# One decode step of a gated attention and MLP block: the first load of wq as two transfers, of 16 and of 112 partitions

## The chip, the cores and the metric

The kernel runs on one core of a Trainium2 chip. The time of a run is in device microseconds, from launch to end on that core. Beside the times of plain runs there is one execution taken by the hardware profiler, with a trace of every instruction and of every data transfer.

## The reference

For two batch rows of one token each, the reference mixes an attention block over a long cache with a small MLP block by a gate:

```
x = A_x                                               # (2, 1, 1024)
g = sigmoid((x * gate_w).sum(-1, keepdims=True))
q = (x @ wq)                                          # wq (1024, 4096): 32 heads of 128
scores = q . k_cache * 128 ** -0.5                    # 4 kv heads, 32768 keys each, 8 q heads to a kv head
a = (softmax(scores) . v_cache) @ wo                  # wo (4096, 1024)
hs = spatial shift of gelu(layernorm(x) @ w1) @ w2    # one token: every shift moves it out, hs = 0
b = x1 + gelu(layernorm(x1) @ w3) @ w4, x1 = x + hs   # w3 (1024, 3584), w4 (3584, 1024)
out = g * a + (1 - g) * b
```

All numbers are 32-bit floats. The two caches are 134 MB each, wq and wo 16.8 MB each, w3 and w4 14.7 MB each. Each of these bytes is used once.

## The kernel before

The kernel is a stream of large loads into two buffers, `bufs[0]` and `bufs[1]` (line 86), each of 128 partitions by 16,384 floats, so 64 KiB (65,536 bytes) in each partition. One load fills one buffer, and loads alternate between the two. There are 40 of them: two each for wq, w3 and w4, then for each of the eight pairs of a kv head and a batch row two of keys (`kt`) and two of values (`vt`), and two of wo. A load of wq, kt, vt or wo is 128 rows of 65,536 bytes, 8.4 MB; one of w3 or w4 has rows of 57,344 bytes.

All these loads are issued by SyncE (SP). The helper `load(i, src, needs)` (lines 469 to 473) makes SP wait until TensorE (PE) has done the work `needs` on what lay in the buffer, and then issues one transfer, which raises the semaphore `landed[i % 2]` by 16 when all of it has landed. The loop of lines 475 to 490 calls it with i = 0, 1, 2 and so on. The loads 0 and 1 (both of wq) wait for nothing. Line 491 calls it once more for the first load of wo, with the literal 0 for i, since that load goes into `bufs[0]`. The second load of wo is written out in lines 492 to 498: five transfers of 8, 4, 2, 1 and 1 sixteenths of the columns, each with a semaphore of its own.

On PE, `take(sem, n)` (line 131) waits for a semaphore and counts it down again by n. `columns` (line 148) takes `landed` and then multiplies the buffer with x: one call for each load of wq and of w3. After the first has read the whole of `bufs[0]`, the event `load0` lets SP issue load 2. The loop over the eight pairs (line 213) takes `landed` before the scores and before the values of each half, lines 280 to 291 do so for wo. Ahead of the first `columns`, PE transposes x, sums for the gate and the layer norm, and puts x * (1 - g) into the accumulator `acc`, with `x16` loaded by a small transfer of 16 partitions from ScalarE's queue (line 140). VectorE (DVE) and ScalarE (ACT) do the softmax, the copies out of PSUM and the norm. At the end DVE copies `acc` (line 462) and SP stores it (line 500).

Of the kernel before, what the change touches and what calls it, by code (L numbers as in the profile page):

```python
# [57 lines left out]
def kernel(  # L58
# [11 lines left out]
    nc = tc.nc  # L70
    scale = DH ** -0.5

    def sbuf(name, cols, rows=P):
        return ctx.enter_context(nc.sbuf_tensor(name, [rows, cols], F32))[:, :]
# [4 lines left out]
    def at(t, offset, *dims, rows=(0, P)):  # L79
        width = t.ap[0][0]  # L80
        return bass.AP(t.tensor, t.offset + rows[0] * width + offset,
                       [[width, rows[1] - rows[0]], *[list(d) for d in dims]])
# [3 lines left out]
    bufs = [sbuf("buf0", RUN), sbuf("buf1", RUN)]  # L86
# [34 lines left out]
    with tc.tile_critical(no_gpsimd_drain=True):  # L121
        new = tc.alloc_semaphore
        landed = [new("landed0"), new("landed1")]
        pieces = [landed[1]] + [new(f"piece{i}") for i in range(1, len(PIECES))]
        edge, dvp, acp = new("edge"), new("dve_to_pe"), new("act_to_pe")
        dve, act = Line(nc.vector, new("dve")), Line(nc.scalar, new("act"))
        pool, sp = Line(nc.gpsimd, new("pool")), Line(nc.sync, None)
# [3 lines left out]
        def take(sem, n=1):  # L131
            t.wait_ge(sem, n).then_inc(sem, -n)  # L132

        def mm(o, lhsT, rhs, start, stop):
            return t.matmul(o, lhsT, rhs, start=start, stop=stop, skip_group_check=True)  # L135

        def quarter(t_, g):
            return t_[C * g:C * g + C]
# [6 lines left out]
        def mark(name, ins):  # L145
            events[name] = pe.did(ins)

        def columns(load, pad, n, banks):
            wide = n // G
            take(landed[load % 2], 16)  # L150
            for ek in range(E * E):
                for u, bank in enumerate(banks):
                    lo, hi = u * 512, min(u * 512 + 512, wide)
                    for g in range(G):
                        start = ek * n + g * wide
                        last = mm(quarter(bank, g)[:, :hi - lo], at(pad, ((load % 2) * 4 + ek) * C, (1, C)),
                                  bufs[load % 2][:, start + lo:start + hi],
                                  load % 2 == 0 and ek == 0, load % 2 == 1 and ek == 3)
            mark(f"load{load}", last)
# [19 lines left out]
        for e in range(E):  # L179
            for kk in range(E):  # L180
                for g in range(G):
                    lo, hi = halves[g % 2]
                    mm(quarter(acc, g), xr_pad[lo:hi, ((g // 2) * 4 + e * 2 + kk) * C:][:, :C],
                       place[lo:hi, P + 1 - P * kk - e:][:, :D // G], e == 0 and kk == 0, False)
        columns(0, x_pad, HQ * DH, sc[0:2])
        columns(1, x_pad, HQ * DH, sc[0:2])
        take(dvp)
# [214 lines left out]
        for half, (lo, hi) in enumerate(halves):  # L402
            for W in range(2):
                n = E * KT
# [64 lines left out]
        def load(i, src, needs):  # L469
            if needs:  # L470
                sp.wait(pe, needs)
            n = src.shape[1]
            nc.sync.dma_start(bufs[i % 2][:, :n], src).then_inc(landed[i % 2], 16)

        i = 0
        for src in (wq, w3, w4):
            for W in range(2):
                load(i, tiles(src, W), events[f"load{i - 2}"] if i > 1 else 0)
                i += 1
        for m in range(PAIRS):  # L480
            for kind, src in (("k", kt), ("v", vt)):
                for L in range(2):
                    if kind == "v":
                        needs = at_pair(m, f"scores{2 * L + 1}")
                    elif m:
                        needs = at_pair(m - 1, f"values{L}")
                    else:
                        needs = events[f"load{4 + L}"]
                    load(i, tiles(src[m], L), needs)
                    i += 1  # L490
# [42 lines left out]
```

## Time and profile before

| | |
|---|---|
| three plain runs, median (lowest to highest) | 777.53 us (777.21 to 777.81) |
| the profiled execution, its own time | 777.37 us |
| its span, first to last instruction | 775.6 us |
| read from HBM | 331.36 MB |
| busy: PE, DVE, ACT, POOL | 433.6, 71.5, 37.2, 4.1 us |
| mean granted TensorE clock | 0.75 |

The page counts the span in microseconds. Matmuls show under PE, the loads of their weights under PEld, and SPq and ACTq are the queues that issue transfers. In the windows, "DMA share" is the mean busy share of the 16 DMA engines and "GB/s" the bytes moved, both booked at the time at which a packet starts. So in windows shorter than a packet they show when packets start, not how fast they run. "x" and a number is a count. In the timeline, square brackets hold the idle time before a group and what ended it. In the order listings a row is an instruction with its shape, and "waits" names the semaphores that it waits for.

### The profile page before, as it was taken

The numbers are of one execution on the slowest core, as the hardware profiler recorded it, in microseconds if no ns is written. First come the engines' busy times: TensorE is split into PE (matmuls) and PEld (weight loads), VectorE is DVE, ScalarE is ACT, GpSimd is POOL, SyncE is SP. The second block draws the span as 40 slices with busy tenths as digits, with TensorE's granted clock in tenths as the row PEclk, the third lists the DMA queues.
The fourth block names the chain that finished last, engine by engine and source line by source line (L and its number), as shares of the span: only waits on it lengthen the run. The fifth ranks groups of instructions, "written<-read, shape, count | busy, mean of one in ns | idle before, by whom it ended". The sixth has DMA issues, their size and how long they took to land. (4 is left out here: it accounts for less than half of the span.)

```text
span 775.6 us, 8888 instructions
## 1 busy us (share of the span) xinstructions
PE 433.6 (56%) x4148; PEld 185.3 (24%) x4148; DVE 71.5 (9%) x203; ACT 37.2 (5%) x88; POOL 4.1 (1%) x14
## 2 busy tenths in 40 slices
PE   4454654483657364835484657464735484657365
PEld 3121231141213121412141213121312141214133
DVE  3000100020002000200020002000200020001000
ACT  1000100020002000200020002000200020002000
POOL 2000000000000000000000000000000000000000
PEclk9976676686679677867686679677967686679679
DMA  9999999999999999999999999999999999999996
GB/s 379 437 432 456 433 419 437 433 434 430 439 436 433 433 433 436 433 433 433 433 430 433 433 433 433 433 433 433 433 436 433 433 433 433 433 433 433 433 423 258
DMA packets 6397, 331.56 MB, mean 428 GB/s; under 512 B 728, under 2 KB 752, under 8 KB 1008
## 3 DMA queue, kind: packets, MB, share of 16 engines
q1 hardware_dynamic: 6352, 331.36, 98.9%
q8 instruction: 10, 0.16, 0.1%
q14 instruction: 3, 0.02, 0.0%
q10 hardware_dynamic: 32, 0.01, 0.0%
HBM read 331.36 MB, written 0.01 MB: 427 GB/s over the span
## 5 line engine op out<-in xcount | busy, mean ns | idle before, releaser
L135 PE MATMUL sc<-buf,q_cur 128*32 128x512 f32 x1024 | 150.7, 754 | 132.2 <-PEq L132 132.2
L135 PE MATMUL pv<-buf,pt 128*32 128x512 f32 x1024 | 133.9, 682 | 102.2 <-PEq L132 102.2
L135 PEld LDWEIGHTS sc<-buf,q_cur 128*32 128x32 f32 x1024 | 41.1, 135 | 235.7 <-issue 235.7
L135 PEld LDWEIGHTS pv<-buf,pt 128*32 128x32 f32 x1024 | 38.9, 123 | 184.2 <-issue 184.0
L417 DVE TENSOR_REDUCE mx<-sc 128x1 f32<-128x512 f32 x32 | 22.1, 691 | 292.8 <-PE sc L135 292.8
L430 ACT ACTIVATE p<-sc,bias 128x512 f32<-128x512 f32 x32 | 21.6, 685 | 563.6 <-DVE bias L427 563.6
L135 PE MATMUL tr<-ident,p 128*64 128x64 f32 x1024 | 43.0, 262 | 9.2 <-PEq L132 9.2
L135 PEld LDWEIGHTS tr<-ident,p 128*64 128x64 f32 x1024 | 42.1, 174 | 9.7 <-issue 9.7
L135 PE MATMUL tr<-sel,pv_sb 128*128 128x8 f32 x128 | 20.1, 294 | 12.0 <-PEq L132 12.0
L135 PE MATMUL sc<-buf,x_pad 128*32 128x512 f32 x128 | 17.5, 708 | 16.7 <-PEq L132 16.7
L450 DVE COPY pv_sb<-pv 128x512 f32<-128x512 f32 x16 | 10.3, 685 | 164.5 <-PE pv L135 164.5
L135 PE MATMUL acc<-buf,h_pad 128*32 128x256 f32 x224 | 16.1, 456 | 14.7 <-PEq L132 14.7
L135 PEld LDWEIGHTS tr<-sel,pv_sb 128*128 128x128 f32 x128 | 19.6, 241 | 19.0 <-issue 19.0
L135 PE MATMUL sc<-buf,xn_pad 128*32 128x384 f32 (+1 forms) x128 | 15.7, 654 | 14.3 <-PEq L132 14.3
L135 PE MATMUL acc<-buf,o_pad 128*32 128x256 f32 x256 | 16.7, 411 | 10.4 <-PEq L132 10.3
L135 PEld LDWEIGHTS acc<-buf,h_pad 128*32 128x32 f32 x224 | 8.9, 131 | 21.5 <-issue 18.6
L135 PEld LDWEIGHTS acc<-buf,o_pad 128*32 128x32 f32 x256 | 9.2, 118 | 17.5 <-issue 14.4
L135 PEld LDWEIGHTS sc<-buf,x_pad 128*32 128x32 f32 x128 | 4.9, 128 | 29.3 <-issue 29.3
L135 PEld LDWEIGHTS sc<-buf,xn_pad 128*32 128x32 f32 x128 | 5.0, 131 | 24.4 <-issue 24.4
L445 DVE RECIPROCAL norm<-tr 128x8 f32<-128x8 f32 x8 | 1.7, 207 | 66.9 <-PE tr L135 66.9
L433 DVE COPY pt<-tr 128x512 f32<-128x512 f32 x8 | 5.5, 691 | 20.6 <-PE tr L135 20.6
L227 PE MATMUL tr<-ident,m 128*1 128x128 f32 x8 | 2.2, 269 | 8.8 <-PEq L132 8.8
(78 smaller groups left out, 100.9 us busy)
## 6 DMA issues: line engine op xcount, KB each, us to landing
buf<-w SPq DMA_DIRECT2D x4, 7168.0 KB, 25.8
buf<-wo SPq DMA_DIRECT2D x1, 4096.0 KB, 20.4
buf<-wo SPq DMA_DIRECT2D x1, 2048.0 KB, 25.0
buf<-wo SPq DMA_DIRECT2D x1, 1024.0 KB, 27.0
buf<-wo SPq DMA_DIRECT2D x2, 512.0 KB, 28.1
buf<-kt SPq DMA_DIRECT2D x16, 29.8
buf<-vt SPq DMA_DIRECT2D x16, 29.1
buf<-wq SPq DMA_DIRECT2D x2, 32.2
```

Source lines behind the costliest of these rows:

```text
L135: return t.matmul(o, lhsT, rhs, start=start, stop=stop, skip_group_check=True)
L227: mark("mt", t.transpose(tr[0][:1, :P], m1[0], ident))
L417: dve.did(v.reduce_max(out=mx[i2][:, i:i + 1], in_=sc[i], axis=AX.X))
L430: act.did(s.activation(p_sb[i], sc[i], AF.Exp, bias=bias[i2], scale=scale, accum_out=l4[i2][:, i:i + 1]), acp)
L433: dve.did(v.tensor_copy(p_t[0], tr[0]), dvp)
L445: dve.did(v.reciprocal(norm, tr[0][:, :REP]))
L450: dve.did(v.tensor_copy(at(pv_sb, e * P, (E * P, G), (H, 2), (1, H)), at(pv, e, (P, G), (0, 2), (2, H))), dvp if e else None)
```

## The change

A new semaphore `first` is made. In `load`, the case i == 0 issues two transfers in place of one: partitions 0 to 15, which raises `first`, and partitions 16 to 127, which raises `landed[0]`. Ahead of the first `columns`, PE takes `first` as well. All other loads go as before.

```
+        first = new("first")
...
+        take(first, 16)
         columns(0, x_pad, HQ * DH, sc[0:2])
...
             n = src.shape[1]
+            if i == 0:
+                nc.sync.dma_start(bufs[0][:16, :n], src[:16]).then_inc(first, 16)
+                nc.sync.dma_start(bufs[0][16:, :n], src[16:]).then_inc(landed[0], 16)
+                return
             nc.sync.dma_start(bufs[i % 2][:, :n], src).then_inc(landed[i % 2], 16)
```

Line 491 of before also calls `load` with 0, so the condition holds there too.

SP's queue at the head of the program, before:

```order
L529 UNCONDITIONAL_BRANCH [waits SP_sequencer_49]
L473 DMA buf<-wq 128x16384 x2
L473 DMA buf<-w 128x14336 [waits pe] x4
L473 DMA buf<-kt 128x16384 [waits pe] x2
L473 DMA buf<-vt 128x16384 [waits pe] x2
```

The same place now (line numbers are those of the changed kernel):

```order
L535 UNCONDITIONAL_BRANCH [waits SP_sequencer_49]
L476 DMA buf<-wq 16x16384
L477 DMA buf<-wq 112x16384
L479 DMA buf<-wq 128x16384
L479 DMA buf<-w 128x14336 [waits pe] x4
```

The first of the two transfers of 128 partitions has become one of 16 and one of 112; the second stands behind them.

SP's queue at the end, where wo is loaded, before:

```order
L473 DMA buf<-wo 128x16384 [waits pe]
L496 DMA buf<-wo 128x8192 [waits pe]
L496 DMA buf<-wo 128x4096
L496 DMA buf<-wo 128x2048
L496 DMA buf<-wo 128x1024 x2
```

And now:

```order
L476 DMA buf<-wo 16x16384 [waits pe]
L477 DMA buf<-wo 112x16384
L502 DMA buf<-wo 128x8192 [waits pe]
L502 DMA buf<-wo 128x4096
L502 DMA buf<-wo 128x2048
```

The first load of wo is in two as well. Nothing takes `first` there.

## The prediction

> **What bounds the kernel now.** I read the page's head and its DMA rows first:
>
> ```profile
> span 775.6 us, 8888 instructions
> PE 433.6 (56%) x4148; PEld 185.3 (24%) x4148; DVE 71.5 (9%) x203; ACT 37.2 (5%) x88; POOL 4.1 (1%) x14
> DMA  9999999999999999999999999999999999999996
> q1 hardware_dynamic: 6352, 331.36, 98.9%
> ```
>
> No engine is near full. The 16 DMA engines are: SP's queue q1 keeps them busy for 98.9% of the span, and only the last of the 40 slices shows slack. The kernel is one stream of bytes, and what lengthens the stream lengthens the kernel. The chain of waits reaches back only over the last microsecond, so it says nothing here.
>
> Next, windows cut to a fraction of a microsecond at the start, and one long window of the middle (the last two columns are DMA share and GB/s):
>
> ```profile
> 1.90:2.90 1.00, 0.00 (x0) 0.00 (x0) 0.73 (x4) 0.73 (x1) 1.00 (x4) 1.00 3.16 1061
> 2.90:4.90 2.00, 0.00 (x0) 0.00 (x0) 2.00 (x4) 0.00 (x0) 2.00 (x5) 1.00 0.00 0
> 4.90:5.70 0.80, 0.34 (x2) 0.37 (x2) 0.54 (x5) 0.00 (x0) 0.18 (x1) 1.00 3.02 1311
> 5.70:7.30 1.60, 1.60 (x10) 1.60 (x9) 0.00 (x0) 0.00 (x0) 0.00 (x0) 1.00 0.00 0
> 7.30:8.10 0.80, 0.80 (x5) 0.80 (x6) 0.00 (x0) 0.00 (x0) 0.00 (x0) 1.00 3.02 1311
> ...
> 100.00:700.00 600.00, 338.92 (x3123) 139.37 (x3119) 55.71 (x150) 27.69 (x70) 0.00 (x0) 0.73 1.00 434
> ```
>
> Packets are booked where they start, and they start in waves. One wave is 0.80 us x 1311 GB/s = 1.05 MB, which is 16 rows of 65,536 bytes: one for each DMA engine. Between waves nothing starts. A row's pace comes from the wave's share: 3.02 x 0.80 us = 2.42 us that each engine spends on its row, and the next wave begins 2.4 us later. So there are 16 streams, each moving one row into one partition at a time, in 2.42 us. A load of 128 rows is eight waves, 8 x 2.42 = 19.4 us. In the long window the share is 1.00 at 434 GB/s, or 27.1 GB/s for each stream, and 65,536 bytes at that rate take 2.42 us again. The first wave begins at about 1.9 us, is 1.0 us wide, and its rows take longer (the second begins 3.0 us after it).
>
> Then the transfers from issue to landing; the first line is that of wq alone (least, median, most):
>
> ```profile
> DMA to landing us min/median/max: 21.9/32.2/42.4
> ...
> buf<-kt SPq DMA_DIRECT2D x16, 29.8
> buf<-vt SPq DMA_DIRECT2D x16, 29.1
> ...
> buf<-wo SPq DMA_DIRECT2D x1, 31.4
> ```
>
> A load in the middle lands 29 to 30 us after its issue, of which 19.4 us are its own rows. It stood about 10 us in the queue (12.0 us for the first of wo). The streams are always fed, with 10 us to spare.
>
> Last the two places that the change touches, in the timeline:
>
> ```profile
> 0.95 0.87 SPq L473 DMA_DIRECT2D buf<-wq  x2
> 23.01 8.85 PE L135 MATMUL sc<-buf,x_pad 128*32 128x512 f32 x64 [4.65 <-PEq L132]
> 31.93 0.33 SPq L473 DMA_DIRECT2D buf<-w  x1
> 43.92 1.94 PE L135 MATMUL sc<-buf,x_pad 128*32 128x512 f32 x8 [12.06 <-PEq L132]
> ...
> 718.75 0.33 SPq L473 DMA_DIRECT2D buf<-wo  x1
> 740.89 2.23 SPq L496 DMA_DIRECT2D buf<-wo  x5
> 750.33 8.75 PE L135 MATMUL acc<-buf,o_pad 128*32 128x256 f32 x128 [5.47 <-PEq L132]
> 768.85 1.86 PE L135 MATMUL acc<-buf,o_pad 128*32 128x256 f32 x24 [0.54 <-PEq L132]
> 771.32 0.64 PE L135 MATMUL acc<-buf,o_pad 128*32 128x256 f32 x8 [0.61 <-PEq L132]
> 772.02 0.42 DVE L462 COPY o_sb<-acc 128x256 f32<-128x256 f32 x1 [26.93 <-PE acc L135]
> ```
>
> PE waits for both loads of wq and for wo, down to the last piece, and what follows the last landing is 0.64 us of PE, 0.42 us of DVE and a store.
>
> **The change part by part.**
>
> *The cheap edits.* One more issue on SP costs about 0.43 us at the start (0.87 for two) and 0.33 us at wo. Behind it stand load 1 at the start, which has 19.4 us of rows ahead of it, and at wo the pieces of line 496, which wait for PE until 740.89 anyway. Without that cover an issue would cost its 0.3 to 0.4 us. The added take of `first` stands on PE where PE has already idled 4.65 us. Queued behind it are the 64 matmuls of load 0, then load 2's issue, which has 10 us to spare; a take with its wait costs at most 0.54 us (the smallest idle in the rows above), and nothing where the other transfer lands later. I count these at nothing.
>
> *The start.* Could 16 rows go off sooner than 128? The first wave is 1.0 us wide, and its rows take about 0.6 us more than 2.42. If every stream began at 1.90 and ran at full pace, the second wave's latest start, 5.70, would be 4.32: a gain of 1.4 us at the utmost. The waves keep their shape for the rest of the run, so this would arrive at the end in full. I take 0, since nothing in the rows ties the width of the first wave to the number of rows issued.
>
> *Where the rows go.* This decides. The bytes are the same, and 16 rows over 16 streams are one row each, 112 are seven each, in sum the eight of before. But in the wave of the first transfer all 16 streams write into 16 neighbouring partitions. No large transfer of before writes fewer than 128 partitions, so the trace can't say whether 2.42 us for a row is the pace of the stream that carries it or of the place into which it is written. Bounds for the transfer of 16: one row for each stream, 2.4 us, if the pace is the stream's own; 8 x 2.42 = 19.4 us, if the way in is divided evenly over the partitions (16 of 128 have two of sixteen shares, for sixteen rows). Between them lie four and eight shares, for 9.7 and 4.8 us. I take 9.7 us: four rows behind each other at each way in, near the middle of the doublings.
>
> [...]
>
> For the transfer of 112, bounds again: 7 x 2.42 = 16.9 us if no two streams ever meet at a way in, and twice that, 33.9 us, if each row shares it with another. Seven rows for a stream don't fall on the same borders as the eight of the full load, so I expect meetings, but not everywhere, and take the middle, 25.4 us.
>
> *The sum.* The first load: 9.7 + 25.4 = 35.1 us in place of 19.4, so 15.7 us more. Nothing hides it: the streams run at a share of 1.00 from then on, PE finishes load 0 later by as much, load 2 is issued later by as much, and the last stream never runs dry. Streams that came through sooner may run dry for a while, which costs nothing, since the latest stream sets the end. The first load of wo is split the same way, another 15.7 us, and the five pieces queue behind it. Both: 31.4 us. The profiled execution took 777.37 us around its span of 775.6; the median of the runs is 777.53, which I start from, as the two differ by 0.02%. 777.5 + 31.4 = 808.9, say **809 us**. By the lower bound of the second transfer a load costs 9.7 + 16.9 - 19.4 = 7.2 us, so 792 for both; by the upper 9.7 + 33.9 - 19.4 = 24.2 us, so 826.
>
> **The rivals.**
>
> *The pace is the stream's own (no change).* Then 2.4 + 16.9 = 19.4 us, as before, and 777.5 us is the time, give or take the 0.4 us of an issue. For it: the steady 27.1 GB/s of each stream, the same for rows of every load. Against: that is seen only where each load spreads over all partitions, where the two explanations look alike. It decides if the wave of 16 rows takes below about 3 us. Chance 0.21.
>
> *The start tightens (faster).* The pace is the stream's own, and besides, the streams start together because the first transfer has one row for each of them. Place: the first wave. Price: at most -1.4 us, so 776.1. This kernel's measurement can tell 0.2% from no change, which is 1.55 us; to be called faster the start would have to give more than the rows allow. It decides only if the first wave narrows from 1.0 us to almost nothing and its rows reach 2.42 us. Chance 0.04, for what I have not seen.
>
> *Neighbouring rows on neighbouring streams, all through.* If the transfer of 112 deals its rows out one at a time, then in each of its seven waves the 16 streams again write 16 neighbouring partitions: 7 x 9.7 = 67.9 us, 77.6 for the load, 58.2 more, and 116 for both: 894 us. For it: it is the simplest way to deal. Against: dealt so, the full loads of before would crowd the same way, and they run at 434 GB/s; only another dealing for 112 than for 128 would bring it. Chance 0.08.
>
> That the wo load stays whole is no rival: the order listing shows it as two.
>
> **How the numbers follow.** The forecast, a crowd at the way in at 7 to 24 us for each load, has a chance of 0.67, and its own range is 792 to 826. With the stream's own pace at 0.21, the range has to reach down to it: from 776.1 (the best start) to 826. Left out are the crowd all through (0.08) and the corner of a second transfer dearer than its upper bound. Faster: 0.04. Same: 0.21. Slower: 0.67 + 0.08 = 0.75.
>
> **What would show it.** In the profile after, the windows at the start: by the forecast, the second wave doesn't begin near 4.9 us but around 11 to 12, and the first matmul on wq near 39 us in place of 23.01. The transfer of 16 partitions would show some 10 us from start to landing. In the middle, 100 to 700 us, the share stays 1.00 or close and nothing else moves except by the delay. At the end the first matmuls on wo come another 10 to 25 us later against the last values. If the second wave begins near 4.9 us, the forecast is wrong at its root. If it begins at 11 us, but the first load lands by 31 us, then only the price of the 112 was too high. If the wo load lands without a delay of its own, the second term is wrong.

## The result and the profile after

| | before | after |
|---|---|---|
| median of plain runs (lowest to highest) | 777.38 us (777.10 to 777.81, 6 runs) | 825.68 us (824.15 to 826.56, 6 runs) |
| profiled execution: its time, its span | 777.37, 775.6 us | 824.88, 823.1 us |

The ratio is 1.0619, with a 95% interval of 1.0607 to 1.0630: 48.3 us slower. The forecast was 809, 31.4 us slower, in a range from 776 to 826. So the time lies inside the range, but 0.3 us from its end, and the slowest of the six runs lies beyond it.

The head of the page after, with the GB/s of the 40 slices (20.6 us each):

```profile
span 823.1 us, 8891 instructions
...
DMA  9999999999999999999999999999999999999995
GB/s 163 264 426 430 416 441 441 427 438 428 431 433 433 433 433 440 427 443 424 443 427 440 427 440 427 440 427 440 427 443 420 446 420 446 424 443 229 229 266 242
...
q1 hardware_dynamic: 6384, 331.36, 98.8%
```

The GB/s row of before, in slices of 19.4 us:

```profile
GB/s 379 437 432 456 433 419 437 433 434 430 439 436 433 433 433 436 433 433 433 433 430 433 433 433 433 433 433 433 433 436 433 433 433 433 433 433 433 433 423 258
```

The same 331.36 MB, a busy share of 98.8% where it was 98.9%, and yet 48 us more. The busy row hides the loss: a slow row counts as busy for as long as it takes (below, 8.5 us for a row of the first wave, where 2.42 us was the pace). The GB/s row shows it. After, the first two slices and the last four fall to between 163 and 266, and all between them run at some 430. Before, only the first and the last slice were low, at 379 and 258. Both loads that were split have their price, and nothing else has.

The windows at the start of after, cut to the waves (rows are booked where they start):

```profile
1.90:3.10 1.20, 0.00 (x0) 0.00 (x0) 0.93 (x4) 0.74 (x1) 1.20 (x5) 1.00 7.10 884
3.10:9.40 6.30, 3.57 (x16) 3.48 (x16) 2.69 (x7) 0.00 (x0) 1.98 (x4) 1.00 0.00 0
9.40:11.70 2.30, 0.58 (x3) 0.55 (x3) 1.18 (x8) 0.00 (x0) 0.00 (x0) 1.00 2.36 456
11.70:15.40 3.70, 1.21 (x10) 0.90 (x14) 0.86 (x5) 1.66 (x3) 0.00 (x0) 1.00 0.00 0
15.40:16.70 1.30, 1.30 (x16) 0.67 (x12) 0.00 (x0) 0.00 (x0) 0.00 (x0) 1.00 3.56 807
20.10:21.30 1.20, 0.00 (x0) 0.00 (x0) 0.00 (x0) 0.00 (x0) 0.00 (x0) 1.00 2.61 874
23.30:25.70 2.40, 0.00 (x0) 0.00 (x0) 0.00 (x0) 0.00 (x0) 0.00 (x0) 1.00 1.59 437
27.00:29.40 2.40, 0.00 (x0) 0.00 (x0) 0.00 (x0) 0.00 (x0) 0.00 (x0) 1.00 1.91 437
31.10:33.90 2.80, 0.00 (x0) 0.00 (x0) 0.00 (x0) 0.00 (x0) 0.00 (x0) 1.00 1.66 374
35.90:38.50 2.60, 0.00 (x0) 0.00 (x0) 0.00 (x0) 0.00 (x0) 0.00 (x0) 1.00 1.73 403
40.50:43.30 2.80, 0.00 (x0) 0.00 (x0) 0.00 (x0) 0.00 (x0) 0.00 (x0) 1.00 1.06 375
100.00:700.00 600.00, 330.83 (x3203) 139.61 (x3199) 57.02 (x162) 29.74 (x73) 0.00 (x0) 0.76 1.00 433
```

In each wave's window 16 rows start (GB/s x width is 1.05 MB), so share x width is the mean time of one row. The first wave, the 16 rows of the first transfer, starts within 1.2 us, and a row takes 7.10 x 1.20 = 8.5 us. The seven waves of the 112 take 5.4, 4.6, 3.1, 3.8, 4.6, 4.6 and 4.5 us, 30.7 us in sum. The last window is the first wave of load 1 at 3.0 us. Before, a row took 2.42 us (3.2 in the first wave). The middle is as before: a share of 1.00 at 433 GB/s.

Transfers from issue to landing (the first line is wq: the 16, the 112 and load 1), and the two places in the timeline:

```profile
DMA to landing us min/median/max: 12.1/42.9/61.8
...
buf<-kt SPq DMA_DIRECT2D x16, 30.1
buf<-vt SPq DMA_DIRECT2D x16, 29.5
```

```profile
1.41 0.42 SPq L477 DMA_DIRECT2D buf<-wq  x1
...
44.46 8.39 PE L136 MATMUL sc<-buf,x_pad 128*32 128x512 f32 x64 [26.09 <-PEq L133]
...
740.36 0.42 SPq L477 DMA_DIRECT2D buf<-wo  x1
...
799.60 13.17 PE L136 MATMUL acc<-buf,o_pad 128*32 128x256 f32 x192 [26.58 <-PEq L133]
820.00 0.70 SPq L506 DMA_DIRECT2D out<-o_sb  x1
```

The first matmul on wq starts at 44.46 in place of 23.01, 21.5 us later. The first on wo starts at 799.60 in place of 750.33, 49.3 us later. The 112 of wo took 59 us from issue to use, where the whole load took 31.6 us (718.75 to 750.33). Keys and values land in 30 us as before.

### The profile page after: what moved, and what is told of

Read it like the earlier page. It is cut to its first block, busy times and chain, and to the rows that moved or that the text cites. A ratio compares the mean times of both kernels' runs of the same rounds, so it can differ in the third digit from the quotient of the medians.

```text
span 823.1 us, 8891 instructions
## 1 busy us (share of the span) xinstructions
PE 422.5 (51%) x4148; PEld 181.3 (22%) x4148; DVE 71.5 (9%) x203; ACT 37.2 (5%) x88; POOL 4.1 (0%) x14
## 3 DMA queue, kind: packets, MB, share of 16 engines
q1 hardware_dynamic: 6384, 331.36, 98.8%
HBM read 331.36 MB, written 0.01 MB: 403 GB/s over the span
## 5 line engine op out<-in xcount | busy, mean ns | idle before, releaser
L136 PE MATMUL sc<-buf,q_cur 128*32 128x512 f32 x1024 | 144.6, 728 | 139.0 <-PEq L133 139.0
L136 PE MATMUL pv<-buf,pt 128*32 128x512 f32 x1024 | 129.7, 664 | 116.1 <-PEq L133 116.1
L432 ACT ACTIVATE p<-sc,bias 128x512 f32<-128x512 f32 x32 | 21.5, 685 | 564.0 <-DVE bias L429 564.0
L136 PE MATMUL tr<-sel,pv_sb 128*128 128x8 f32 x128 | 17.1, 269 | 12.0 <-PEq L133 12.0
L136 PEld LDWEIGHTS tr<-sel,pv_sb 128*128 128x128 f32 x128 | 16.6, 209 | 19.0 <-issue 19.0
L136 PEld LDWEIGHTS sc<-buf,xn_pad 128*32 128x32 f32 x128 | 5.1, 135 | 24.2 <-issue 24.2
L435 DVE COPY pt<-tr 128x512 f32<-128x512 f32 x8 | 5.5, 692 | 19.1 <-PE tr L136 19.1
L439 DVE COPY pt<-tr 128x512 f32<-128x512 f32 x8 | 5.5, 692 | 18.8 <-PE tr L136 18.8
```

What stands on the lines that cost most here:

```text
L432: act.did(s.activation(p_sb[i], sc[i], AF.Exp, bias=bias[i2], scale=scale, accum_out=l4[i2][:, i:i + 1]), acp)
L435: dve.did(v.tensor_copy(p_t[0], tr[0]), dvp)
L439: dve.did(v.tensor_copy(p_t[2], tr[0]), dvp)
```

## The experiments

Theory A is that of the prediction: rows of one wave crowd into too few ways in. Its rivals are B (only the tail hurts), C (more transfers cost time) and D (the side that is read is slow). All kernels start from the kernel before.

### One split at a time: wq_only and wo_only

```
 def load(i, src, needs, split=False): ...
+            if split:
+                nc.sync.dma_start(bufs[0][:16, :n], src[:16]).then_inc(first, 16)
+                nc.sync.dma_start(bufs[0][16:, :n], src[16:]).then_inc(landed[0], 16)
+                return
```

In wq_only, `split` is set for the first load of wq alone; in wo_only for the first load of wo alone, and PE takes `first` there.

> Only the first load of wq is split into 16 and 112 partitions; the first load of wo is one transfer, as before. Theory A (the rows of a wave crowd into too few partitions, and the streams stand behind each other where they write): the first load lands some 21 us later than the 22.9 us of before, as it does in the changed kernel, and the delay reaches the end whole: 777.4 + 21 = 798 us. Rival B (only the tail is hurt, since a delay at the start is caught up by the queue's 10 us of spare time): under 785 us. Rival C (the price is that of more transfers in the queue, not of partitions): the same 21 us, so this run doesn't tell A from C.

> Only the first load of wo is split into 16 and 112 partitions, and TensorE takes both semaphores there; wq is as before. Theory A with each load paying for itself: another 21 us, 798 us, and the two single splits then add up to 42 of the 48 us that the changed kernel lost, the last 6 us being what the streams, staggered by the first split, add at the second. If the load of wo is dearer in itself (it runs beside the end of vt and the pieces): 27 us, 804 us, and the two add up to 48.

wq_only: 797.84 us, ratio 1.0263 (1.0246 to 1.0280), against 777.32 of before. wo_only: 801.96 us, 1.0321 (1.0304 to 1.0338). The splits cost 20.5 and 24.6 us. Rival B falls: the delay at the head arrives whole. The two add up to 45.2 of the 48.3 us. The split of wo is the dearer one alone, by 4 us, between the two prices that I had named.

### The same sizes, cut the other way: columns

```
+                nc.sync.dma_start(bufs[0][:, :2048], src[:, :2048]).then_inc(first, 16)
+                nc.sync.dma_start(bufs[0][:, 2048:n], src[:, 2048:]).then_inc(landed[0], 16)
```

> Both first loads (wq and wo) come as two transfers of the same sizes as in the changed kernel, 1.05 and 7.34 MB, but cut by columns: 2,048 and 14,336 columns of all 128 partitions. Theory A: each wave again writes all over the partitions, so no price: 777.4 us, within 1 us. Rival C (a second transfer, its issue, its completion or its size cost the time): near 825 us, or at least 10 us more than before.

777.10 us against 777.32, ratio 0.9998 (0.9988 to 1.0007): no change. The landings of the two transfers of wq in its profile (KB, us):

```profile
buf<-wq SPq DMA_DIRECT2D x1, 7168.0 KB, 21.1
...
buf<-wq SPq DMA_DIRECT2D x1, 1024.0 KB, 4.6
```

1.05 MB over 128 partitions lands in 4.6 us, over 16 partitions in 12.1. So neither the second transfer nor its issue, its completion or the added take costs anything that can be measured. Rival C falls.

### Written side or read side: nb_nb, sp_sp, sp_nb, nb_sp

The first load of wq comes as eight transfers of 16 rows, r = 0 to 7. "nb" stands for neighbours, "sp" for every eighth; the first half of a name is the partitions written, the second the rows read.

```
nb_nb  bufs[0][16 * r:16 * r + 16, :n] <- src[16 * r:16 * r + 16]
sp_sp  bufs[0][r:r + 121:8, :n]        <- src[r:r + 121:8]
sp_nb  bufs[0][r:r + 121:8, :n]        <- src[16 * r:16 * r + 16]
nb_sp  bufs[0][16 * r:16 * r + 16, :n] <- src[r:r + 121:8]
```

> The first load of wq comes as eight transfers of 16 neighbouring partitions each, from 16 neighbouring rows; wo as before. Theory A (crowding where the rows are written): every wave stands four deep, about 9.3 to 9.7 us each, 75 to 77 us in place of 19.4, so 777.4 + 55 to 58 = 832 to 835 us. Rival C (only the number and size of transfers): small. Rival D (neighbouring rows are slow to read at one time): also 832 to 835 us.

> Eight transfers of 16 rows as in nb_nb, but each takes every eighth row and writes every eighth partition. Theory A: rows eight partitions apart share a way in less often; by the price of the halves (64 partitions in two transfers cost 21 us) I expect two deep, 38.7 us for the load, 797 us. Rival C (number of transfers): the same time as nb_nb. Rival D: rows far apart in memory, no price, 778 us.

> Eight transfers of 16 rows; each reads 16 neighbouring rows but writes every eighth partition, so the rows of wq come to other partitions than the reference wants. Theory A: the time of sp_sp, 797 us, since only the written side counts. Rival D (the read side): the time of nb_nb, 832 to 835 us.

> Eight transfers of 16 rows; each reads every eighth row but writes 16 neighbouring partitions, so again the rows of wq come to other partitions than the reference wants. Theory A: the time of nb_nb, 832 to 835 us. Rival D (the read side): the time of sp_sp, 797 us or less.

| | reads neighbours | reads every eighth |
|---|---|---|
| writes neighbours | nb_nb 832.88 us, 1.0717 (1.0686 to 1.0748) | nb_sp 832.10 us, 1.0707 (1.0676 to 1.0738) |
| writes every eighth | sp_nb 798.62 us, 1.0276 (1.0247 to 1.0306) | sp_sp 798.69 us, 1.0277 (1.0248 to 1.0307) |

Each is the median of two plain runs, against 777.16 us of before. The second and the third wave of nb_sp, and of sp_nb:

```profile
9.60:11.95 2.35, 0.83 (x4) 0.80 (x4) 1.05 (x8) 0.00 (x0) 0.00 (x0) 1.00 3.96 446
18.90:21.30 2.40, 0.00 (x0) 0.00 (x0) 0.00 (x0) 0.00 (x0) 0.00 (x0) 1.00 3.88 437
```

```profile
6.70:7.90 1.20, 1.20 (x7) 1.20 (x7) 0.00 (x0) 0.00 (x0) 0.00 (x0) 1.00 4.27 874
...
11.80:13.00 1.20, 0.43 (x2) 0.34 (x2) 0.42 (x3) 0.52 (x2) 0.00 (x0) 1.00 4.27 874
```

By share x width a row into 16 neighbours takes 9.3 us (3.8 times 2.42), and one into every eighth partition 5.1 us (2.1 times), whatever rows are read. The time follows the written side to within 0.8 us, and rival D falls. 1.05 MB in 9.3 us are 113 GB/s, 0.26 of the 434 GB/s of whole loads. No run counts the ways in.

### Halves, and thirty-two: halves and w32

```
halves  bufs[0][:64, :n] <- src[:64], then bufs[0][64:, :n] <- src[64:]
w32     bufs[0][:32, :n] <- src[:32], then bufs[0][32:, :n] <- src[32:]
```

> The first load of wq comes as two transfers of 64 partitions; wo as before. Theory A, by the measured price of 16 neighbours (four times a row's pace, so four ways in for 16 partitions): if 64 partitions have half of the ways in, each stream shares its way with one other, rows take 4.8 us, and the load takes 38.7 us in place of 19.4: 797 us. If 64 partitions reach them all, no price: 777 to 778 us. Rival C: small, since the transfers are large, under 780 us. [...]

> The first load of wq comes as transfers of 32 and 96 partitions, two and six neighbouring rows for each stream. If a wave in which any streams share a way costs all streams double (4.84 us): eight such waves, 38.7 us in place of 19.4, 797 us. If only the streams that share are slowed and the others run ahead: about 13 to 14 us more, 791 us. If 32 partitions reach enough ways in for 16 streams: less, 785 us or below.

halves: 798.47 us, 1.0272 (1.0255 to 1.0289), 21.1 us more. w32: 797.75 us against 777.53, 1.0260 (1.0243 to 1.0277), 20.2 us more. The third and fourth wave of w32, the first two of its 96 rows:

```profile
11.70:13.50 1.80, 0.55 (x2) 0.46 (x2) 0.51 (x3) 1.00 (x2) 0.00 (x0) 1.00 2.63 583
16.40:18.40 2.00, 1.97 (x20) 0.66 (x12) 0.00 (x0) 0.00 (x0) 0.00 (x0) 1.00 2.54 524
```

The mean row takes 4.7 and 5.1 us over all 16 streams, about double 2.42. The 791 us that I expected if only the sharing streams slowed are 7 us off; which streams share, no run shows. That the rows of one stream are neighbours isn't shown for 32 and 96 either; the next section shows it for 112. The expectation of a wave that costs all streams double as soon as some share a way, 797 us, is met within 1 us. It doesn't hold for every wave, as the last section shows.

### The 112 written out by hand: seven

```
bufs[0][:16, :n] <- src[:16]
bufs[0][16 + r:r + 122:7, :n] <- src[16 + r:r + 122:7]     # r = 0 to 6
```

> The first load of wq comes as the transfer of partitions 0 to 15 and then seven transfers of 16 rows each, which take and write every seventh partition: 16, 23, 30 and so on, then 17, 24, 31 and so on. This writes out by hand what the transfer of 112 would do if each of the 16 streams got seven neighbouring rows and took them in order. If it is dealt so: the time of wq_only, 797.8 us, within 1 us, and the same waves (about 5.2, 4.6, 2.9, 3.7, 4.6, 4.6, 4.4 us). If the 112 are dealt one row at a time in turn, this kernel differs: each wave of the 112 would be 16 neighbours, so wq_only would cost like nb_nb, which it does not. Any other dealing: another time than 797.8, or other waves.

797.41 us against 777.53, 1.0259 (1.0241 to 1.0276), where wq_only has 1.0263. Its waves two, three, four, five and six:

```profile
9.30:11.80 2.50, 0.68 (x3) 0.65 (x3) 1.25 (x9) 0.00 (x0) 0.00 (x0) 1.00 2.16 419
15.50:16.60 1.10, 1.10 (x16) 0.65 (x12) 0.00 (x0) 0.00 (x0) 0.00 (x0) 1.00 4.34 953
20.30:21.30 1.00, 0.00 (x0) 0.00 (x0) 0.00 (x0) 0.00 (x0) 0.00 (x0) 1.00 3.17 1049
23.50:26.00 2.50, 0.00 (x0) 0.00 (x0) 0.00 (x0) 0.00 (x0) 0.00 (x0) 0.50 1.54 419
27.40:29.50 2.10, 0.00 (x0) 0.00 (x0) 0.00 (x0) 0.00 (x0) 0.00 (x0) 0.50 2.12 499
```

5.4, 4.8, 3.2, 3.9 and 4.5 us, against 5.4, 4.6, 3.1, 3.8 and 4.6 in the changed kernel. With the same time and the same cheap fourth and fifth wave, the 112 rows behave as seven neighbours for each stream, taken in order. A whole load of 128 can't be dealt as eight neighbours for each stream in the same way: sp_sp writes that out by hand and costs 21.5 us (798.69 against 777.16), where the whole load's rows take 2.42 us each. How a whole load is dealt, no run here shows. In the dear waves, here and in the changed kernel, the mean row takes 4.5 to 5.4 us, about what 16 rows at twice the pace, 4.84 us, would give. Had a few rows alone been slow, say four at 4.84 us and twelve at 2.42, the mean would be 3.0 us, an estimate from the pace of 2.42; the fourth wave comes near that, with 3.2 us here and 3.1 there.

### Why wo costs more: second and wo_late

In second, the split is of the second load of wq, into `bufs[1]`. In wo_late, wo_only's split load waits longer:

```
-        load(0, tiles(wo, 0), at_pair(PAIRS - 1, "values0"), True)
+        load(0, tiles(wo, 0), at_pair(PAIRS - 1, "values1"), True)
```

> The second load of wq, not the first, is split into 16 and 112 partitions. The streams have a full load ahead of it and are at most 0.8 us apart, where at wo they are 2.4 us apart. If the split of wo costs 24.6 us (against 20.5 for the first load of wq) because rows of the load ahead are held up too: 802 us here as well. If because the streams are further apart there, so that the crowded wave lasts longer: near 798 us here.

> As wo_only, but SP issues the split load of wo only after TensorE has done the last values (values1 in place of values0), some 22 us later. By then the streams are empty, and they start on the 16 rows together, as at the head of the program; the kernel pays for the idle time. If the split of wo costs 24.6 us instead of 20.5 because the streams are some 2 us apart there: the transfer of 112 lands 43 to 44 us after its issue, as at the head of the program in wq_only (44.1), and the time is 777.4 + 12.6 of idle streams (issue at 740.9, 21.9 to land, against 750.2) + 20.5 to 21.5 = 810.5 to 811.5 us. If the load of wo is dearer in itself: 47 to 48 us from issue to landing, and 814 to 815 us.

second: 798.54 us against 777.53, 1.0276 (1.0258 to 1.0293), 21.0 us more: a full load ahead in the queue adds nothing of note. wo_late: 809.84 us against 777.32, 1.0416 (1.0399 to 1.0434), about 1 us under what I expected of streams that start together, and over 4 us under the other case. The issue of the 112 in wo_late, and PE's first use of wo:

```profile
740.86 0.42 SPq L477 DMA_DIRECT2D buf<-wo  x1
```

```profile
784.31 8.39 PE L136 MATMUL acc<-buf,o_pad 128*32 128x256 f32 x128 [39.45 <-PEq L133]
```

From issue to use are 43.5 us. At the head of wq_only the transfers of wq (the 16, the 112, load 1) land so long after their issue:

```profile
DMA to landing us min/median/max: 12.4/44.1/63.1
```

The 112 take about as long at both places (43.5 and 44.1 us). The 16 rows of wo_late start together again, within 0.9 us, and take 8.6 us each:

```profile
741.40:742.30 0.90, 0.39 (x4) 0.42 (x4) 0.37 (x1) 0.00 (x0) 0.00 (x0) 1.00 9.54 1165
```

How far the streams are apart before, at the place of wo:

```profile
718.90:719.70 0.80, 0.12 (x2) 0.03 (x1) 0.44 (x2) 0.00 (x0) 0.00 (x0) 1.00 0.57 246
719.70:720.50 0.80, 0.00 (x0) 0.00 (x0) 0.00 (x0) 0.00 (x0) 0.00 (x0) 1.00 1.14 492
720.50:721.30 0.80, 0.00 (x0) 0.00 (x0) 0.00 (x0) 0.00 (x0) 0.00 (x0) 1.00 1.33 573
```

3, 6 and 7 rows start in the three windows: one wave is spread over 2.4 us, where it was 0.8 us wide at the head. With the streams brought together, the load of wo pays the price of wq: 809.84 less 777.32 and less the 12.6 us estimated for idle streams leaves 19.9 us, where wq_only lost 20.5. So the 4 us don't come from wo itself (wo_late), nor from a load ahead in the queue (second). Streams that are apart are what is left, by elimination; no run sets their distance alone.

## Why the prediction was right, and where it was short

**Right: what bounds the kernel.** The stream of bytes sets the end, the delay at the head arrives there whole (20.5 us in wq_only), and the 10 us of spare queue cover none of it.

**Right: the cheap edits.** More issues, takes and completions together cost nothing (columns: -0.2 us, inside its interval).

**Right: no gain at the start.** The 16 rows of the first wave of after spread over a window of 1.2 us, where the first 16 of 128 took 1.0 us.

**Right: where the rows are written decides, at close to four times a row's pace.** The 16 rows take 8.5 us in the first wave and 9.3 in a steady one, for 9.7 forecast. No row of before led to four; I took it as near the middle between one and eight, so by the rows alone it was a guess that hit. Exchanging what is read and what is written showed the side. With that the rivals of the stream's own pace and of the tighter start fall: a row took 8.5 us where they had 2.4.

**Too small: the transfer of 112.** I took 25.4 us, the middle of 16.9 and 33.9. The waves measure 30.7, and load 1's first wave another 0.6 above 2.42. The step that failed is "Seven rows for a stream don't fall on the same borders as the eight of the full load, so I expect meetings, but not everywhere, and take the middle": where such borders lie and how many streams meet in a wave, no run shows, but in five of the seven the mean row of the wave took 4.5 to 5.4 us, 1.9 to 2.2 times 2.42. The 39.8 us of 8.5 + 30.7 + 0.6 stand against 20.1 us before, as the first wave of before took 3.2 us (3.16 x 1.00) and not the 2.42 that the forecast's 19.4 counts for it. That makes 19.7 us for wq, where wq_only lost 20.5 and the forecast had 15.7.

**Too small: the same price for wo.** Alone it costs 24.6 us. By elimination (second, wo_late) the extra 4 us come from streams that stand 2.4 us apart there. Both splits together cost another 3 us or so that neither costs alone; the intervals of the three measurements reach 0.9 to 1.3 us to each side, so the size is loose. Streams further apart after the first split would be the nearest explanation, but the trace of after has no sign of it. In three windows like those above, ahead of the rows of wo, its rows start so:

```profile
743.10:743.90 0.80, 0.00 (x0) 0.00 (x0) 0.00 (x0) 0.00 (x0) 0.00 (x0) 0.74 0.76 328
743.90:744.70 0.80, 0.00 (x0) 0.00 (x0) 0.00 (x0) 0.00 (x0) 0.00 (x0) 0.50 0.76 328
744.70:745.50 0.80, 0.00 (x0) 0.00 (x0) 0.00 (x0) 0.00 (x0) 0.00 (x0) 0.50 1.51 655
```

These are 4, 4 and 8 rows, one wave spread over 2.4 us, as in the kernel before. Where the 3 us come from is open.

So of the 16.9 us by which the forecast was short, 4.8 lie in wq, 8.9 in wo and some 3 in the two together.

**Luck: that the time stayed inside the range.** The upper end, 826, counts 24.2 us for each load. The load of wq cost 20.5, and that room was taken up by the 4 and the 3 us of wo, for which the prediction had no term. The signs named in the prediction say the same: the second wave began at 9.40 us, not at 11 to 12, the first matmul on wq came at 44.46 for 39, and that on wo came another 27.8 us later, for 10 to 25.

The rival of neighbouring rows all through, 58 us for a load, exists as nb_nb (55.7 us); the kernel's own 112 rows are dealt otherwise, as seven shows.

## What to carry to other kernels

Where loads bound the kernel, look at which partitions a transfer fills, not only at its size: here an 8.4 MB load of wq cut by partitions into 16 and 112, 32 and 96 or 64 and 64 cost 20 to 21 us, and two loads cut by columns cost nothing. Loads of other sizes weren't run. Read the GB/s of the slices beside the busy share, since here the share stayed at 98.8% while slices fell to 163 GB/s. And look at which calls a condition like `i == 0` meets: half of the price here came from the load of wo.

## What the runs showed that I had not expected

Whole waves are slow: in five of the seven waves of the 112 the mean row took 4.5 to 5.4 us where 2.42 is the pace, about as much as in sp_nb (5.1 us). Which streams meet in such a wave, and whether the others wait as well, is open. Not every wave does this. The fourth wave of after, at 3.1 us the cheapest of the seven, looks like this when it is cut in three:

```profile
20.10:20.99 0.89, 0.00 (x0) 0.00 (x0) 0.00 (x0) 0.00 (x0) 0.00 (x0) 1.00 1.86 663
20.99:21.03 0.04, 0.00 (x0) 0.00 (x0) 0.00 (x0) 0.00 (x0) 0.00 (x0) 1.00 19.17 4915
21.03:21.30 0.27, 0.00 (x0) 0.00 (x0) 0.00 (x0) 0.00 (x0) 0.00 (x0) 1.00 2.61 971
```

By GB/s x width these are 9, 3 and 4 rows; share x width x 16, divided by the rows, gives 2.9, 4.1 and 2.8 us for a row. So here a few rows are slow and the others nearly keep their pace. And the prediction took the waves to keep their shape for the rest of the run, but the streams drift apart, from 0.8 us in the first waves to 2.4 us at wo. In the middle that costs nothing (434 GB/s); at wo it goes with the dearer split.
